# Attention and gated MLP on one core: from the eighth pair on, row maxima without a bias pass on TensorE; the attention run of a pair unbroken; setup off VectorE; maxima written in place

## The chip, the core and the metric

The kernel runs on one NeuronCore of a Trainium2 chip. Its five engines (TensorE, VectorE, ScalarE, GpSimd, and SyncE, which here issues all transfers) run their own instruction queues in order and wait for one another by semaphores. The metric is the device time of one launch in microseconds (us). In the profile TensorE is PE (its weight loads PEld), VectorE DVE, ScalarE ACT, GpSimd POOL, SyncE SP.

## The reference

Causal attention with a position bias over 8 batches x 8 heads, 576 positions, head size 64, and behind it a gated MLP with a depthwise convolution of width 3.

```python
scores = scale * np.matmul(q, k.transpose(0, 1, 3, 2))
cum = np.cumsum(np.maximum(s, 0.0), axis=-1)
bias = -(cum[:, :, :, None] - cum[:, :, None, :])
scores = np.where(causal, -1000000000.0, scores + np.minimum(bias, 0.0))
scores = scores - np.max(scores, axis=-1, keepdims=True)
attn = np.exp(scores)
attn = attn / (np.sum(attn, axis=-1, keepdims=True) + 1e-09)
x = attn @ v                                  # heads side by side: (8, 576, 512)
h = np.maximum(x @ w_in, 0.0)                 # w_in (512, 1024)
conv_out[:, t] = sum over k of conv_w[k] * h[:, t + k - 1]
out = (h * sigmoid(conv_out)) @ w_out         # w_out (1024, 512)
```

`cum` does not fall along a row, so under the causal mask the bias of a query is `cum[key] - cum[query]`.

## The kernel before

**Pairs.** Two heads make a pair; there are 32 pairs (p = 0 to 31), four to a batch. The two heads lie in partitions 0 to 63 and 64 to 127 and are worked on by matmuls with 64 rows each, two side by side. For each pair:

- `qk`, `hi`, `lo`: q and k are loaded and split into a leading and a rest part (`raw` to `s`); ACT or DVE makes the first, POOL the second.
- `sh0` to `sh3`: q k^T with queries in partitions, in four pieces of 288, 288, 448+64 and 320+192 columns, each for two heads in two of the six PSUM banks `ps0` to `ps5` (`sh_mm`). A first pass multiplies q and k, a second pass adds the keys' bias (tile `eb` times `ek`). `mx` (`sh_max`) takes the row maxima on DVE, in 12 operations per pair: a plain reduction, or a custom operation that adds a mask and takes the maximum, followed by a read of its accumulator. The custom operation writes its sum to a bf16 tile `junk` that nobody reads.
- `tn`, `rt`, `ds`: the maxima are transposed on PE, and go by DMA into a row of `eq`.
- `sc0` to `sc3`: k q^T with keys in partitions, three passes on the split parts and one of bias and maximum (`eq`, `ek`); `ex` is the exponential on ACT, `mk` the causal mask on POOL (from pair B0 = 9 on; before it, extra small matmuls on PE add the mask).
- `ad`, `sum`, `pv`: column sums and attn times v, on PE in column tiles of 32.
- `gd`, `inv`, `ri`, `rb`, `nm`: the sums (128 x 144) go through ACT, a reciprocal on DVE, a DMA to DRAM, a DMA that spreads them over the partitions, and a product on DVE. Then `xh`, `xl` split x.

**MLP.** For each batch and half, `h` (12 matmuls each, L1315) and after ReLU, convolution and gate `o` (6 matmuls each, L1442). At the start w_in and w_out arrive as words of 8 bytes and are rebuilt on DVE, ACT and POOL.

**Order.** A scheduler inside the kernel (`Sched.play`) plays all tasks through once, with a cost for each, a due time (its formula plus a table of shifts, `DUE`) and the free buffers, and writes each engine's instructions in the order that comes out. For pairs from B0 on the list `ORDER` says in which order the PE tasks of a pair follow; `sh` of the next pair runs with `sc` of this one. A "|" in it ends a burst, and only between bursts may `h`, `o` and `tn` come in. PE changes between three ways of tiling: 64 rows (`sh`, `sc`), 32 columns (`sum`, `pv`, `tn`) and the full array (`h`, `o`).

**The other way to maxima.** The code has a second way for pairs from `RB` on (`late` in `pair`): the row `cum` of both heads is loaded into all partitions (`rw`, 128 x 2 x 576, one tile), POOL cuts off keys behind the query in it (`cut_off`, five selects per pair, of which that for tau = 3, 2, 1 waits for the maxima of tau + 1, because they write over the columns that these read), and `sh_max` adds that row to q k^T. Its PE pass with `eb` and `ek` is left out. With RB = 32 no pair takes it.

Of the kernel before, what the change touches and what calls it, by code (L numbers as in the profile page):

```python
# [1556 lines left out]
```

## Time and profile before

| | |
|---|---|
| median of 3 runs | 785.36 us (784.96 to 786.0) |
| profiled execution | 785.74 us, of which the span in the trace is 783.9 us |
| PE busy | 746.5 us, 95% |
| DVE busy | 561.4 us, 72% |
| ACT busy | 446.7 us, 57% |
| POOL busy | 334.4 us, 43% |
| moved by DMA | 62.33 MB |

Busy is the time in which at least one instruction of the engine ran. Matmuls overlap, so what one costs is read from the distance of starts, not from its own duration. A row of the timeline has its start, its length, the engine, the line, the operation, output and inputs, and in brackets the idle time before it with what ended it.

### The profile page before, as it was taken

The page shows a single profiled execution, that of the slowest core. Times are in us where ns is not written, and L with a number is a line of the kernel's source. Part 1 is how long each engine was busy: PE and PEld are TensorE (multiplying, and loading weights), DVE is VectorE, ACT ScalarE, POOL GpSimd, SP SyncE. Part 2 cuts the span into 40 slices and gives each one's busy share as a digit, 9 for nine tenths or more (in the row PEclk, how much of TensorE's full clock was granted, in tenths as well). Part 3 has the DMA queues.
Part 4 walks back from the last instruction along what each step waited for, and adds up shares of the span by engine and source line. Part 5 has one row for each costly group of instructions (what it writes and reads, how often), then busy time and mean ns, then how long its engine had stood idle before and what let it go on. Part 6 is the DMA issues. An engine that isn't in the chain of part 4 may idle for free.

```text
span 783.9 us, 19117 instructions
## 1 busy us (share of the span) xinstructions
PE 746.5 (95%) x7528; PEld 616.8 (79%) x7528; DVE 561.4 (72%) x1355; ACT 446.7 (57%) x908; POOL 334.4 (43%) x456
## 2 busy tenths in 40 slices
PE   0898999999999999999999999999999999999998
PEld 0677788888888788787878788787887878888986
DVE  8986889753778685777776867777777768866532
ACT  4655565645656465665655566666655655644533
POOL 3343644412444455456254444545335354342311
PEclk9998999999999999999999999999999999999999
DMA  8364541211122312122222221222222121111001
GB/s 279 124 202 141 160 127 55 65 47 60 37 84 81 98 45 73 53 84 82 68 68 82 82 77 53 83 84 83 68 73 84 57 53 50 51 33 34 27 28 42
DMA packets 45466, 62.33 MB, mean 80 GB/s; under 512 B 5312, under 2 KB 30208, under 8 KB 45376
## 3 DMA queue, kind: packets, MB, share of 16 engines
q1 hardware_dynamic: 45376, 61.10, 25.3%
q8 instruction: 59, 0.97, 0.5%
q14 instruction: 31, 0.25, 0.1%
HBM read 48.83 MB, written 12.09 MB: 78 GB/s over the span
## 4 chain that ended last, share of the span: by engine, by line
PE 81%; DVE 7%; DMA 5%; issue 3%; ACT 2%; POOL 1%; SPq 1%; DVEq 0%; ACTq 0%; POOLq 0%
PE ps L1315 26%; PE ps L1442 25%; PE ps L1109 12%; PE pv L1163 9%; PE ps L991 6%; PE ps L1217 3%; DMA ri_d<-rs 2%; DMA rb<-ri_d 2%; DVE junk L1022 1%; DMA ht<-w_out 1%; ACT pt L1126 1%; DVE ad L1180 1%; DVE ct L1371 1%; DVE rs L1241 1%; DVE r L1013 1%
## 5 line engine op out<-in xcount | busy, mean ns | idle before, releaser
L1315 PE MATMUL ps<-x,wi 128*128 128x258 f32 (+1 forms) x1536 | 222.1, 300 | 0.9 <-ACT pt L1126 0.5
L1315 PEld LDWEIGHTS ps<-x,wi 128*128 128x128 f32 x1536 | 211.0, 189 | 8.1 <-issue 2.3
L1442 PE MATMUL ps<-wo,u 128*128 128x512 f32 x768 | 196.9, 402 | 0.5 <-ACT pt L1126 0.3
L1126 ACT ACTIVATE pt<-ps,less 128x288 f32<-128x288 f32 (+1 forms) x256 | 137.1, 591 | 78.7 <-PE ps L1109 76.1
L1385 POOL TENSOR_TENSOR u<-ct,u 128x512 fp32r<-128x512 f32 x64 | 84.5, 1321 | 219.8 <-ACT u L1380 167.2
L1352 DVE SCALAR_TENSOR_TENSOR ct<-ht,cw_sb,ct 128x320 f32<-128x320 f32 (+3 forms) x256 | 137.0, 542 | 50.2 <-ACT ct L1338 45.5
L1442 PEld LDWEIGHTS ps<-wo,u 128*128 128x128 f32 x768 | 138.6, 188 | 33.2 <-issue 3.0
L1109 PE MATMUL ps<-s 64*128 64x288 f32 (+4 forms) x1152 | 118.3, 309 | 2.0 <-ACT pt L1126 0.8
L1138 POOL TENSOR_SCALAR_AFFINE_SELECT pt<-pt 128x128 f32<-128x128 f32 x230 | 64.1, 302 | 116.0 <-ACT pt L1126 113.4
L1109 PEld LDWEIGHTS ps<-s 64*128 64x128 f32 (+1 forms) x1152 | 82.7, 177 | 25.1 <-issue 7.6
L1022 DVE CUSTOM_DVE_ANT_0 junk<-ps,mask 128x448 bf16<-128x448 f32 (+3 forms) x184 | 77.8, 423 | 29.4 <-PE ps L991 14.6
L1326 ACT ACTIVATE ht<-ps 128x257 f32<-128x257 f32 (+1 forms) x128 | 52.3, 410 | 78.5 <-PE ps L1315 75.1
L897 POOL TENSOR_TENSOR s<-raw,s 128x1152 fp32r<-128x1152 f32 x31 | 85.0, 2743 | 23.3 <-issue 13.2
L1163 PE MATMUL pv<-pt,v 128*32 128x448 f32 (+4 forms) x1536 | 94.0, 391 | 0.0
L1163 PEld LDWEIGHTS pv<-pt,v 128*32 128x32 f32 x1536 | 51.6, 111 | 40.0 <-issue 28.6
L991 PE MATMUL ps<-s 64*128 64x288 f32 (+4 forms) x384 | 65.5, 319 | 10.4 <-DVE s L891 3.9
L1180 DVE TENSOR_TENSOR ad<-ad,pt 128x192 f32<-128x192 f32 (+2 forms) x131 | 63.9, 541 | 8.0 <-POOL pt L1138 7.8
L1338 ACT ACTIVATE ct<-ht,cw_sb 128x320 f32<-128x320 f32 (+1 forms) x123 | 65.6, 535 | 5.6 <-ACT ht L1326 0.4
L991 PE MATMUL ps<-ek,eb 64*128 64x288 f32 (+4 forms) x384 | 59.7, 321 | 4.9 <-ACT ek L926 4.9
L1013 DVE TENSOR_REDUCE r<-ps 128x1 f32<-128x288 f32 (+4 forms) x136 | 51.0, 431 | 18.5 <-PE ps L991 18.3
L1371 DVE TENSOR_TENSOR ct<-ct,ht 128x640 f32<-128x640 f32 (+1 forms) x64 | 53.1, 830 | 11.8 <-ACT ct L1365 11.7
L1365 ACT ACTIVATE ct<-ct 128x640 f32<-128x640 f32 (+1 forms) x64 | 43.6, 681 | 24.1 <-DVE ct L1352 23.9
(94 smaller groups left out, 861.3 us busy)
## 6 DMA issues: line engine op xcount, KB each, us to landing
raw<-qk SPq DMA_DIRECT2D x32, 576.0 KB
v<-vp SPq DMA_DIRECT2D x32, 320.0 KB
rb<-ri_d SPq DMA_DIRECT2D x64, 144.0 KB
out<-ob SPq DMA_DIRECT2D x32, 256.0 KB
w<-w_in SPq DMA_DIRECT2D x8, 512.0 KB
ri_d<-rs SPq DMA_DIRECT2D x32, 72.0 KB
ht<-w_out SPq DMA_DIRECT2D x8, 256.0 KB
w<-w_out SPq DMA_DIRECT2D x4, 512.0 KB
```

Of the source, the lines that this page charges most:

```text
L897: tt_on(e)(st[:, i, :], R_t[raw.slot][:, i], st[:, j, :].bitcast(F32), op=ALU.subtract)
L991: nc.tensor.matmul(dst[j], l, m, start=(k == 0), stop=(k == 1 or late))
L1022: nc.vector.tensor_tensor_reduce(out=junk[:, 0 : c1 - c0], in0=bank(pb, o, o + c1 - c0), in1=add_, scale=1.0, scalar=acc if c0 else -3.0e3 ...
L1109: nc.tensor.matmul(d, l, m, start=(k < 2), stop=(k >= len(steps) - 2 or (t == L and k < 2)), skip_group_check=t == L,)
L1126: nc.scalar.activation(PT_t[pts[j].slot][:, o : o + w], bank(pb, 0, w), AF.Sigmoid, bias=less, scale=0.125,)
L1163: nc.tensor.matmul(pvt[gs, o0 : o0 + c1 - c0], vt[0:jt, t, gs], PT_t[pts[g // 2].slot][0:jt, O_T[t] + c0 : O_T[t] + c1], start=(t == 0), s ...
L1180: tt_on(e)(acc, pt[:, P:S] if t == 1 else acc, pt[:, O_T[t] : O_T[t] + W_T[t]], op=ALU.add,)
L1315: nc.tensor.matmul(bank(hb, 0, XW[hf]), l, r, start=(k == 0), stop=(k == len(seq) - 1))
L1338: nc.scalar.activation(o, src, AF.Copy, scale=w)
L1352: nc.vector.scalar_tensor_tensor(cc[:, lo:hi], h_[:, sh + lo : sh + hi], cw_sb[:, 3 * f + k : 3 * f + k + 1], cc[:, lo:hi], op0=ALU.mult, ...
L1385: tt_on(e)(uu[:, 1, i, :], C_t[ct.slot][:, i, k0:hw], uu[:, 0, i, :].bitcast(F32), op=ALU.subtract)
L1442: nc.tensor.matmul(bank(pb, 0, DM), l, r, start=(fp == 0 and k == 0), stop=(fp == NF // 2 - 1 and k == len(seq) - 1),)
```

## The change

Seven things change.

1. `RB` goes from 32 to 7: pairs 7 to 31 take their maxima the other way. PE loses for these 25 pairs the pass with `eb` and `ek` (300 of its matmuls), DVE works only with the custom operation, now with the float32 row `rw` as its second input, POOL gets five selects per pair and SP a load of 576 KB per pair, and `rt` adds an offset from a small table `off`.
2. `ORDER` loses its bars and puts `sh0`, `sh1` first: from pair 9 on the attention run of a pair is one burst, with no `h`, `o` or `tn` inside.
3. The custom operation writes its sum over the PSUM bank it reads; `junk` is gone.
4. The setup (constants, masks, pads of `ek`) moves from DVE to POOL and ACT.
5. The sums are folded by DMA from 128 x 144 (eight rows in use) to 128 x 9 before the reciprocal (`fo`, two DMAs per pair), and stored from there.
6. `ek` has two buffers (NE = 2) and one more for the early pairs; `ad` alternates the heads; the two taps of the convolution are tasks of their own.
7. The scheduler's costs and the whole table `DUE` are new, so the order of everything is.

```diff
-NE = 3
+NE = 2
...
-SWITCH = 0.105
+SWITCH = 0.2, 0.095
...
-RB = 32
-ORDER = ("sum", "pv", "sc0", "sh0", "|", "sc1", "sh1", "|", "sc2", "sh2", "|", "sc3", "sh3")
+RB = 7
+ORDER = ("sh0", "sh1", "sum", "pv", "sh2", "sc0", "sc1", "sh3", "sc2", "sc3")
...
     def c_clear(e):
-        nc.vector.memset(ones, 1.0)
-        nc.vector.memset(ncz, 0.0)
...
+        g = nc.gpsimd
+        g.memset(ones, 1.0)
+        g.memset(cols, 0.0)
...
     def c_pads(i):
         def run(e):
-            t = EK_t[i].bitcast(F32)
-            nc.vector.memset(t, 0.0)
-            for j in range(2):
-                nc.vector.memset(t[D * j : D * j + NB + 2, 0:S], -1.0)
-                nc.vector.memset(t[D * j : D * j + NB + 1, S:FW], NEG)
+            v = ident[:, 0:1]
+            for k, (c0, c1) in enumerate(((0, S), (S, FW))):
+                nc.scalar.activation(
+                    EK_t[i][:, c0:c1], bass.AP(v.tensor, v.offset, [v.ap[0], (0, c1 - c0)]),
+                    AF.Identity, bias=cols[:, k : k + 1], scale=0.0,
+                )
...
-                            out=junk[:, 0 : c1 - c0], in0=bank(pb, o, o + c1 - c0),
+                            out=bank(pb, o, o + c1 - c0), in0=bank(pb, o, o + c1 - c0),
...
+        def fold(e):
+            for j in range(2):
+                nc.sync.dma_start(
+                    rc_t[D * j : D * j + D], rs_t[j : j + 97 : 32].rearrange("g (k c) -> g k c", k=16)
+                )
+
+        t_fold = add(f"fo{p}", [("SP", 0.8)], [t_grd], tq, fold, uses=[ri], nbytes=30000)
+
         def inverse(e):
-            nc.vector.reciprocal(rs_t, rs_t)
+            nc.vector.reciprocal(rc_t, rc_t)
```

The order of instructions shows it at two places. First PE, in the middle of the program, before: the end of `sc0`, then `sh0` of the next pair with its second pass (`ek`, `eb`), 12 matmuls of `h`, and `sc1` (L1109 is `sc`, L991 `sh`, L1315 `h`; a row 128x288 stands for one head).

```order
L1109 MATMUL ps0_65<-eq0_87,ek1_85 128x288
L1109 MATMUL ps1_66<-eq0_87,ek1_85 128x288
L991 MATMUL ps2_67<-s0_82 128x288
L991 MATMUL ps4_69<-s0_82 128x288
L991 MATMUL ps2_67<-ek2_86,eb_113 128x288
L991 MATMUL ps4_69<-ek2_86,eb_113 128x288
L1315 MATMUL ps5_70<-x0_93,wi_78 128x322 x12
L1109 MATMUL ps0_65<-s1_83 128x288
L1109 MATMUL ps1_66<-s1_83 128x288
```

The same engine in the changed program, in the run of one pair: the end of `sc0`, `sc1` in two other banks, `sh3` of the next pair in a bank of `sc0`, and `sc2` (L1142 is `sc`, L1024 `sh`).

```order
L1142 MATMUL ps2_67<-eq0_85,ek1_84 128x288
L1142 MATMUL ps3_68<-eq0_85,ek1_84 128x288
L1142 MATMUL ps4_69<-s0_81 128x288
L1142 MATMUL ps5_70<-s0_81 128x288
...
L1142 MATMUL ps4_69<-eq0_85,ek1_84 128x288
L1142 MATMUL ps5_70<-eq0_85,ek1_84 128x288
L1024 MATMUL ps2_67<-s1_82 128x320
```

The second pass is gone, and so is the MLP work between the pieces; a bank is written again after one other piece. In the whole program the stretches with one way of tiling fall from 225 (96 of them with 64 rows) to 143 (66), when `tn` is counted with the full array.

Second POOL, before: masks of the probabilities (L1138), one sum (L1180), splits of x (L1281) and the split of the next q and k (L897).

```order
L1138 AFFINE_SELECT pt1_92<-pt1_92 64x64
L1180 TENSOR_TENSOR ad_96<-pt0_91 128x448
L1281 TENSOR_TENSOR x0_93<-rb_95,x0_93 128x322
L1281 TENSOR_TENSOR x1_94<-rb_95,x1_94 128x258
L1138 AFFINE_SELECT pt0_91<-pt0_91 128x128 x2
L1138 AFFINE_SELECT pt1_92<-pt1_92 128x128 x2
L1385 TENSOR_TENSOR u1_1860<-ct1_106,u1_1860 128x512
L897 TENSOR_TENSOR s0_82<-raw0_80,s0_82 128x1152
```

And in the changed program, around one pair: L982 is a select of the loaded row, L930 the split, L1434 a split of the MLP, L1173 a mask of the probabilities.

```order
L982 AFFINE_SELECT rw_87<-rw_87 128x2x128
L982 AFFINE_SELECT rw_87<-rw_87 128x2x64
L930 TENSOR_TENSOR s0_81<-raw0_79,s0_81 128x1152
L982 AFFINE_SELECT rw_87<-rw_87 128x2x128
L1434 TENSOR_TENSOR u0_1666<-ct2_108,u0_1666 128x512
L1173 AFFINE_SELECT pt0_91<-pt0_91 128x128
L982 AFFINE_SELECT rw_87<-rw_87 128x2x128
L1173 AFFINE_SELECT pt1_92<-pt1_92 128x128
L982 AFFINE_SELECT rw_87<-rw_87 128x2x128
```

The five selects stand spread over POOL's queue, among its long operations.

## Rows read from the trace of the kernel before

**Rows 1.** Windows: stretch, length, busy us (count) of PE, PEld, DVE, ACT, POOL; PEclk, DMA.

```profile
0.00:25.00 25.00, 4.96 (x44) 3.92 (x45) 22.13 (x56) 12.31 (x20) 10.07 (x17) 1.00 0.82 266
50.00:75.00 25.00, 23.34 (x368) 18.29 (x364) 19.85 (x51) 12.27 (x29) 9.97 (x9) 0.86 0.57 180
200.00:700.00 500.00, 494.59 (x4839) 402.97 (x4838) 368.89 (x928) 295.76 (x602) 239.41 (x371) 1.00 0.24 70
```

**Rows 2.** Timeline of the start: first bias row, on DVE, and PE's first second pass.

```profile
10.05 0.54 DVE L641 TENSOR_SCALAR pt<-pt 64x576 f32<-64x576 f32 x1
...
21.07 0.61 PE L991 MATMUL ps<-ek,eb 64*128 64x288 f32 x2 [4.89 <-ACT ek L926]
```

**Rows 3.** Timeline of PE in one pair's run, in the middle.

```profile
407.27 0.29 PE L991 MATMUL ps<-ek,eb 64*128 64x288 f32 x2
407.49 1.67 PE L1442 MATMUL ps<-wo,u 128*128 128x512 f32 x6
...
409.87 0.30 PE L991 MATMUL ps<-ek,eb 64*128 64x288 f32 x2
410.00 0.78 PE L1109 MATMUL ps<-s 64*128 64x448 f32 x6
...
411.31 0.36 PE L991 MATMUL ps<-ek,eb 64*128 64x448 f32 x2
411.51 0.19 PE L991 MATMUL ps<-s 64*128 64x64 f32 x2
411.54 0.27 PE L991 MATMUL ps<-ek,eb 64*128 64x64 f32 x2
411.65 0.68 PE L1109 MATMUL ps<-s 64*128 64x320 f32 x6
```

**Rows 4.** Chain that ended last, in order of time: start, length, what.

```profile
343.07 1.60 PE ps L1442 x6
...
346.40 1.65 PE ps L1315 x12
348.04 1.40 PE ps L1442 x6
...
349.56 1.45 PE ps L1315 x12
```

**Rows 5.** Groups by shape: count, busy us, mean ns, idle before and its releaser.

```profile
L897 POOL TENSOR_TENSOR s<-raw,s 128x1152 fp32r<-128x1152 f32 x31 | 85.0, 2743 | 23.3 <-issue 13.2 <-ACT s L891 8.0 <-DMA rb<-ri_d 1.1
L1126 ACT ACTIVATE pt<-ps,less 128x288 f32<-128x288 f32 x128 | 56.1, 497 | 50.5 <-PE ps L1109 50.1
L1138 POOL TENSOR_SCALAR_AFFINE_SELECT pt<-pt 128x128 f32<-128x128 f32 x184 | 55.4, 315 | 116.0 <-ACT pt L1126 113.4
L1241 DVE RECIPROCAL rs<-rs 128x144 f32<-128x144 f32 x32 | 33.6, 1050 | 23.7 <-ACT rs L1236 23.7
L1022 DVE CUSTOM_DVE_ANT_0 junk<-ps,mask,r 128x288 bf16<-128x288 f32 x64 | 33.0, 516 | 32.8 <-PE ps L991 27.5 <-DVE r L1022 0.7 <-ACT ek L926 0.2
L1022 DVE CUSTOM_DVE_ANT_0 junk<-ps,mask 128x448 bf16<-128x448 f32 x46 | 28.6, 622 | 12.2 <-PE ps L991 4.8 <-ACT pt L1126 4.2 <-DVE r L1022 0.9
L1180 DVE TENSOR_TENSOR ad<-pt 128x448 f32<-128x448 f32 x21 | 20.9, 1013 | 0.0
L1022 DVE DVE_READ_ACCUMULATOR2_ANT r<- 128x1 f32 x248 | 20.4, 82 | 0.0
L1013 DVE TENSOR_REDUCE r<-ps 128x1 f32<-128x448 f32 x18 | 10.3, 616 | 1.9 <-PE ps L991 1.9
```

**Rows 6.** Timeline of an early pair's four score pieces without MLP work between, PE.

```profile
56.53 0.79 PE L1109 MATMUL ps<-s 64*128 64x448 f32 x6
...
58.09 1.09 PE L1109 MATMUL ps<-s 64*128 64x320 f32 x6 [0.17 <-ACT pt L1126]
```

**Rows 7.** Timeline of SP: store of the reciprocals and the spread that waits for it.

```profile
405.40 0.35 SPq L1246 DMA_DIRECT2D ri_d<-rs  x1
...
407.09 1.29 SPq L1255 DMA_DIRECT2D rb<-ri_d  x2
```

More of the change, by code (lines that the diff above doesn't have):

```diff
@@ L46 @@
 LO1 = 4.0
-LAND = 0.65
+LAND = 0.85
+LEAD = {"PE": 0.0, "DVE": 0.08, "ACT": 0.1, "POOL": 0.04, "SP": 0.0}
+AFTER = {"PE": 0.2, "DVE": 0.12, "ACT": 0.14, "POOL": 0.1}
 ADD_ = 0.0
@@ L376, in play @@
                 else:
-                    post(now + dur + (0.2 if e == "PE" else 0.07), "done", t)
+                    post(now + dur + AFTER[e], "done", t)
             if not events:
@@ L466 @@
     cw_sb = const.tile([P, NF * 3], F32, name="cw_sb")
-    junk = const.tile([P, W_T[1]], BF16, name="junk")
     wi = const.tile([P, 2, NC, DF], F32R, name="wi")
@@ L572, in c_clear, with c_clear2 @@
     def c_clear(e):
-        nc.vector.memset(ones, 1.0)
-        nc.vector.memset(ncz, 0.0)
-        nc.vector.memset(tab[:, 0:1], 0.0)
-        nc.vector.memset(onehot, 0.0)
-        nc.vector.memset(onehot[:, 2:3], 1.0)
-        nc.vector.memset(less, -EK)
+        g = nc.gpsimd
+        g.memset(ones, 1.0)
+        g.memset(cols, 0.0)
+        for j in range(2):
+            g.memset(cols[D * j : D * j + NB + 2, 0:1], -1.0)
+            g.memset(cols[D * j : D * j + NB + 1, 1:2], NEG)
+        g.memset(ncz, 0.0)
+        g.memset(tab[:, 0:1], 0.0)
+    def c_clear2(e):
+        g = nc.gpsimd
+        g.memset(onehot, 0.0)
+        g.memset(onehot[:, 2:3], 1.0)
+        g.memset(less, -EK)
         for r8 in R8_t:
-            nc.vector.memset(r8, 0.0)
-        nc.vector.memset(mrow, 0.0)
-        nc.vector.memset(mask, 0.0)
+            g.memset(r8, 0.0)
+        g.memset(mrow, 0.0)
+        g.memset(mask, 0.0)
     def c_ident(e):
@@ L627 @@
     t_s = add("s", [("SP", 1.2)], [], -200, lambda e: nc.sync.dma_start(s_sb, s), nbytes=147456)
+    t_clear = add("clear", [("POOL", 1.3)], [], -191, c_clear)
     t_ident = add("ident", [("POOL", 1.0)], [], -190, c_ident)
-    t_clear = add("clear", [("DVE", 1.3)], [], -190, c_clear)
-    t_tab = add("tab", [("DVE", 0.3)], [t_ident, t_clear], -189.5, c_tab)
-    t_mrow = add("mrow", [("POOL", 4.0)], [t_clear, t_tab], -188.4, c_mrow)
-    t_tri = add("tri", [("POOL", 0.6)], [t_clear], -188.3, c_tri)
-    t_pads = [add(f"pads{i}", [("DVE", 1.4)], [], -189 + i, c_pads(i)) for i in range(NE)]
+    t_tab = add("tab", [("POOL", 0.3)], [t_ident, t_clear], -189.5, c_tab)
+    t_hot = add("hot", [("POOL", 1.3)], [], -189.4, c_clear2)
+    t_unit = add("unit", [("POOL", 0.35)], [t_ident], -189.3, c_unit)
+    t_mrow = add("mrow", [("POOL", 3.2)], [t_hot, t_unit], -188.4, c_mrow)
+    t_tri = add("tri", [("POOL", 0.3)], [t_hot], -188.3, c_tri)
+    t_pads = [
+        add(f"pads{i}", [("ACT", 1.0)], [t_clear, t_ident], -187 + i, c_pads(i)) for i in range(len(EK_t))
+    ]
     t_eb = add("eb", [("ACT", 0.72)], [t_tab], -188, c_ind(EB_t))
@@ L637 @@
     ]
-    t_hot = t_clear
     def cum_chain(e):
@@ L874, in pair @@
         late = p >= RB
-        raw, sb, vb, ek, eq = buf("raw"), buf("s"), buf("v"), buf("ek"), buf("eq")
+        extra = not late and RB < NP and p % 3 == 2
+        raw, sb, vb, ek, eq = buf("raw"), buf("s"), buf("v"), buf("eke" if extra else "ek"), buf("eq")
         lanes = [slice(D * j, D * j + D) for j in range(2)]
@@ L1173, in pair @@
         if ad:
-            for j in range(2):
-                t_ad = None
-                for t in range(1, NT):
+            t_ads = [None, None]
+            for t in range(1, NT):
+                for j in range(2):
+                    t_ad = t_ads[j]
                     def pre_add(e, j=j, t=t):
@@ L1190, in pair @@
                     )
-                added.append(t_ad)
+                    t_ads[j] = t_ad
+            added = t_ads
         def sums(e):
@@ L1257, in spread @@
                 )
-        t_rb = add(f"rb{p}", [("SP", 1.35)], [t_ri], tq, spread, alloc=[rb], uses=[ri],
+        t_rb = add(f"rb{p}", [("SP", 1.25)], [t_ri], tq, spread, alloc=[rb], uses=[ri],
                    nbytes=438000)
@@ L1343, in moe_h, with tap @@
                       [t_relu, t_cw], h_tag(b, hf, f) + 0.1, center, uses=[ht, ct])
-            def tap(e, i=i, f=f):
-                h_ = H_t[ht.slot][:, i, :]
-                cc = C_t[ct.slot][:, i, :]
-                for k in (0, 2):
+            t_tap = t_c
+            for k in (0, 2):
+                def tap(e, i=i, f=f, k=k):
+                    h_ = H_t[ht.slot][:, i, :]
+                    cc = C_t[ct.slot][:, i, :]
                     sh = hf + k - 1
@@ L1356, in tap @@
                     )
[L1358 to L1359 removed]
+                t_tap = add(f"t{'ab'[k // 2]}{b}.{hf}.{f}", [("DVE", 0.205 + hw / 0.96e3, True)], [t_tap],
+                            h_tag(b, hf, f) + 0.1, tap, uses=[ht, ct])
+            taps.append(t_tap)
         tg = h_tag(b, hf, 2 * fp + 1) + 0.2
```

60 lines of the change are left out of this document (32 added, 28 removed), and 153 rows, old and new, of the table DUE.

## The prediction, on record before the run

> **What bounds the kernel now.** I read the windows first, because a share of 95% over the whole span hides which stage is full. In the 500 us from 200 to 700 PE is busy for 494.6 us, DVE for 369, ACT for 296, POOL for 239 [rows 1]. So there a microsecond that PE no longer has to work is a microsecond of the kernel, unless PE then stands and waits, and the 5.4 us in which it is idle are all that it visibly waits today. The first 25 us are another stage: PE is busy for 4.96 us, DVE for 22.1. The timeline of the start says why. The chain that makes the bias rows starts on DVE at 10.05 us, and PE's first pass with `ek` comes at 21.07, after ACT has levelled a row that had to travel through DRAM [rows 2]. From 50 to 75 us PE is at 23.3 of 25, but its granted clock is 0.86 on average: part of that stretch ran at the lower of the two levels, 1.2 GHz, while DVE worked for 19.9 of the 25 us [rows 1]. In the middle, then, PE's own work bounds the kernel, and at the start DVE and what follows it.
>
> **The sum goes against the profiled execution**, 785.74 us, which is 0.4 above the median of 785.36. About 0.2% (1.6 us) is what a measurement of this kernel can tell from no change.
>
> **The second pass.** Two heads run side by side, so what a pass costs is the distance from its start to the next start. For 288 columns that is 410.00 - 409.87 = 0.13 us, for 448 it is 411.51 - 411.31 = 0.20, for 64 it is 411.65 - 411.54 = 0.11 [rows 3]. A pair has 288 twice, 448, 64, 320 and 192. For the last two, which lie between, I take 0.15 and 0.12. That makes 0.84 us per pair, and 25 pairs give 21 us; if the 64 columns cost only what the first pass of 64 does (411.54 - 411.51 = 0.03), it is 19. Pairs 7 and 8 also lose 28 small mask matmuls: at half of 0.11 us each some 1.5 us, at nothing 0; I take 1.
>
> **The switches of tiling.** Six matmuls of `o` take 1.40 us when PE stays with the full array and 1.60 when 64-row work follows; twelve of `h` take 1.45 and 1.65 [rows 4]. So a switch to 64 rows costs 0.20 us. The other way, the last pass before `o` takes 407.49 - 407.27 = 0.22 instead of 0.13: 0.09 us [rows 3]. The order has 96 stretches of 64 rows before and 66 after, 129 others before and 77 after: 30 x 0.20 + 52 x 0.09 = 10.7, say 11 us. For switches between columns and rows I have no row and use the same two prices; at nothing for them it would be 8 us.
>
> **What the unbroken run costs.** Before, each piece was followed by MLP work in most cases, and a bank had time to be emptied. Now the run goes `sh2`, `sc0`, `sc1`, `sh3`, `sc2`, `sc3` with six banks of which each piece takes two. I count from the start of `sc0`. Its four passes of 288 end at 0.5 us and those of `sc1` at 1.05. The last matmuls take 0.30 us themselves [rows 3], so ACT can start at about 0.8, and two exponentials of 0.50 us [rows 5] free the banks of `sc0` at 1.8. `sh3` wants them at 1.05: 0.75 us of waiting. The custom operations on `sh2` take 0.62 + 0.08 us for 448 columns [rows 5], perhaps 0.3 for 64, all of it twice: 2.0 us, so its banks are free at 2.3, and `sc2`, which would come at about 2.1, waits 0.15 more. That is 0.9 us per burst. An early pair has four score pieces in a row already, and there the fourth waits visibly for 0.17 us, and its first matmuls take 1.09 us, where the same six take 0.68 in the middle [rows 3, 6]: 0.6 us for one such reuse, so the size is right. In the order, 17 of the 23 bursts have six banks. In the other six a bank is still kept by `o`, so that `sc1` waits for `sc0` and `sc3` for `sc2` too; I put 1.9 us there. 17 x 0.9 + 6 x 1.9 = 27; the 5.4 us idle of today are mostly waits of this kind and go: +21 us net. From below it is about nothing (0.3 us per burst, as now), from above 2.0 us in every burst, +41. I take the middle, since the row of the early pair is the nearest.
>
> **Setup off DVE.** If POOL needs as long for its memsets as DVE did, nothing is gained; if the bias chain starts almost at once, 9 us. POOL is busy for only 10 of the first 25 us [rows 1] and the MLP's splits can wait, so I take 5. What covers it is that ACT, which now fills the pads, was busy for 12 of these 25 us.
>
> **The fold.** DVE loses 1.05 us per pair and gets back perhaps 0.2 [rows 5]: 27 us over 32 pairs, of which only those of the early pairs count, where DVE is what PE waits for: 7 x 0.85 = 6 us, at best 8 with the drop of the clock avoided, at least 0. I take 4. For it the chain from the sums to x gets one more DMA. Store to spread takes 407.09 - 405.40 = 1.69 us [rows 7], so the chain grows by 1.69 - 0.85 = 0.85 us. MLP work covers it in the middle; where x is late at the ends of the 8 batches it is 7 us at most.
>
> **What costs nothing.** Custom instead of plain reductions: 0.62 + 0.08 against 0.62 us for 448 columns [rows 5], for some 66 operations under 10 us, on a DVE with 131 of 500 us free. Writing over the bank instead of `junk`: no row shows it; if it cost nothing or as much again as a read of the accumulator, 0.08 us, that is 24 us on DVE at most, under the same cover. The selects: 125, each on twice the 128 columns that take 0.315 us [rows 5], so 40 to 79 us on a POOL with 261 of 500 us free. The loads: 25 x 576 KB = 14.7 MB, on DMA engines that are busy for a quarter [rows 1].
>
> One place shows that the engines are not as free as that. On 448 columns DVE takes 1.01 us with both inputs in SBUF and 0.62 with one in PSUM [rows 5]. The Trainium skill (GPSIMD Engine Reference, section 1, Specifications) says that GpSimd's interfaces to SBUF are shared with VectorE and that they get into each other's way when a DVE instruction has two SBUF inputs. The 0.4 us agree with it. By that rule POOL's added selects and memsets slow the rebuilding of the weights at the start, and the 4 us of the fold are lost: 768 instead of 764. By the rows alone the fold's relief stays. I stay with the rows, since most selects come after the weights are done.
>
> **The sum:** -21 - 1 - 11 + 21 - 5 - 4 = -21; 785.7 - 21 = 764.7, less the 0.4 to the median: 764 us.
>
> **Rivals.**
>
> *The waits stay hidden* (0.17). If ACT and DVE empty the banks as fast as PE comes back, the run costs 0.3 us per burst, about what is idle now: 785.4 - 42 + 2 = 745 us. For it speaks that ACT is busy for only 59% in the middle [rows 1]; against it, the early pair [rows 6].
>
> *POOL comes too late* (0.09), the case on the slower side. The select for tau = 3 waits for the four maxima of `sh0` and `sh1`, and the custom operations on `sh2` wait for it, on an engine that works in order. A split of 2.74 us [rows 5] ahead of that select holds up DVE, `sh2` keeps its banks, and `sc2` stands. From 0.9 us more in each of the 23 bursts on, the gain of 21 us is gone; half a split each time, 1.4 us, gives 785.4 - 21 + 32 = 796 us. POOL is free for half of the middle [rows 1] and the sums and `pv` give it 3 us, which speaks against it.
>
> *x comes late or the start does not move* (0.10). The longer chain at 8 batch ends adds 7 us, or the 9 us of start and fold fail: 771 to 773 us.
>
> *Given back in full* (0.04). The bursts cost 1.9 us everywhere: 23 x 1.9 - 5 = 39, and 785.4 - 42 + 39 = 782; with a little of the last rival within 0.2% of before.
>
> **How the numbers follow.** The forecast (0.60) has its own range of 752 to 776: the waits between 0.4 and 1.4 us per burst. With the hidden waits below and the rivals near it above, 745 to 780 holds 8 in 10. Faster: 0.60 + 0.17 + 0.10 = 0.87; no change 0.04; slower 0.09.
>
> **What would show it.** `ps<-ek,eb` has 84 matmuls, not 384, and PE's count falls by some 330. The first of them starts near 16 us. DVE's reciprocals shrink to about 0.2 us. PE shows idle time before `sh3` and `sc2`, released by the exponentials and by the custom operations, in all some 25 us in the middle; the groups of six `o` at 1.60 us become rare. I am wrong if that idle time is near nothing or over 40 us, if POOL's selects are named as what DVE waited for in most bursts, or if `h` waits for x at the ends of batches.

## The result, and the profile after

| | before | changed | ratio, 95% interval |
|---|---|---|---|
| first comparison, medians of 8 runs each | 785.68 us | 776.89 us | 0.9893 [0.9865, 0.9921] |
| the changed kernel again, later (6 runs) | 785.52 us | 777.98 us | 0.9892 [0.9862, 0.9923] |

The change gives 8 to 9 us, not 21. The profiled execution of the changed kernel took 780.09 us, 2 to 3 more than its median; below, differences between traces are taken from it, and times of experiments go against 777.5 us, between the two medians.

Busy times of the whole span, from the page of the changed kernel:

```profile
PE 726.9 (93%) x7200; PEld 603.6 (78%) x7200; DVE 550.1 (71%) x1475; ACT 443.8 (57%) x880; POOL 369.3 (47%) x557
```

The windows that answer to [rows 1]:

```profile
0.00:25.00 25.00, 4.54 (x38) 3.50 (x40) 17.45 (x34) 13.04 (x24) 15.79 (x35) 1.00 0.88 270
50.00:75.00 25.00, 22.24 (x392) 16.54 (x393) 21.20 (x57) 15.72 (x35) 12.11 (x9) 1.00 0.60 188
200.00:700.00 500.00, 480.96 (x4608) 396.13 (x4607) 371.74 (x1056) 291.58 (x573) 264.63 (x444) 0.99 0.30 93
```

In the middle PE is now idle for 19 us of 500 (before: 5.4), and in the first 25 us it does as little as before, although DVE has 4.7 us less to do. The timeline of the start, from DVE, SP, ACT and PE, says what took DVE's place (it answers to [rows 2]):

```profile
3.85 0.54 DVE L673 TENSOR_SCALAR pt<-pt 64x576 f32<-64x576 f32 x1 [3.85 <-DMA pt<-s]
...
6.17 0.57 DVE L680 TENSOR_SCALAR pt<-pt,v 64x576 f32<-64x576 f32 x1
...
5.76 3.97 SPq L759 DMA_DIRECT2D w<-w_in  x1
9.85 1.32 SPq L696 DMA_DIRECT2D grid_d<-pt  x1
11.27 0.54 SPq L698 DMA_DIRECT2D rest_d<-pt  x1
11.91 0.55 SPq L718 DMA_DIRECT2D ncr_d<-v  x1
12.50 1.01 SPq L719 DMA_DIRECT2D cum_d<-pt  x1
13.60 1.02 SPq L912 DMA_DIRECT2D raw<-qk  x2
15.20 0.66 SPq L945 DMA_DIRECT2D ek<-grid_d  x2
...
20.66 0.78 ACT L959 ACTIVATE ek<-ek,nbt 74x576 fp32r<-74x576 f32 x1 [1.72 <-DMA ek<-grid_d]
...
21.49 0.61 PE L1024 MATMUL ps<-ek,eb 64*128 64x288 f32 x2 [10.68 <-ACT ek L959]
```

The chain starts 6.2 us earlier and its row is ready at 6.74. But SP stands in the issue of a weight load until 9.73, stores the row at 9.85, then does two stores that the new way to maxima needs (`ncr_d`, `cum_d`) and two loads of q and k, and only then the load of `ek`. PE begins at 21.49; before it was 21.07. The same store, load and levelling (ACT) in the kernel before:

```profile
12.79 0.49 SPq L664 DMA_DIRECT2D grid_d<-pt  x1
...
16.23 0.67 SPq L912 DMA_DIRECT2D ek<-grid_d  x2
...
20.25 0.78 ACT L926 ACTIVATE ek<-ek,nbt 74x576 fp32r<-74x576 f32 x1 [4.39 <-DMA ek<-grid_d]
```

So of the 6.2 us the store keeps 2.9, the load 1.0, and the levelled row nothing: from store to load takes 5.35 us instead of 3.44, from load to levelling 5.46 instead of 4.02. The DMA engines are nearly full in this stretch in both traces: in the three windows of 5 us from 5 to 20 us the view gives them a busy share of 1.01, 1.02 and 0.86 before, and 1.00, 1.08 and 0.98 after.

Groups by shape, answering to [rows 5]:

```profile
L1055 DVE CUSTOM_DVE_ANT_0 ps<-ps,rw,r 128x288 f32<-128x288 f32 x50 | 24.2, 521 | 1.2 <-POOL rw L982 1.1
L1055 DVE CUSTOM_DVE_ANT_0 ps<-ps,rw 128x448 f32<-128x448 f32 x50 | 30.4, 647 | 2.4 <-PE ps L1024 0.7 <-POOL rw L982 0.7
L1055 DVE DVE_READ_ACCUMULATOR2_ANT r<- 128x1 f32 x314 | 44.3, 141 | 0.0
L1287 DVE RECIPROCAL rc<-rc 128x9 f32<-128x9 f32 x32 | 6.8, 212 | 17.3 <-DMA rc<-rs 17.1 <-issue 0.2
L982 POOL TENSOR_SCALAR_AFFINE_SELECT rw<-rw 128x256 f32<-128x256 f32 x100 | 52.5, 525 | 109.2 <-DVE r L1055 63.2 <-DMA rw<-cum_d 38.7 <-DVE rc L1287 7.1
L1217 DVE TENSOR_TENSOR ad<-pt 128x448 f32<-128x448 f32 x33 | 22.4, 684 | 3.1 <-POOL pt L1173 3.1
```

**Where the time went, by stretches.** Matmuls of a pair's `sum` mark the pairs. Distances in us from the traces:

| | to pair 0's sum | to pair 8's sum | to pair 31's sum | rest | span |
|---|---|---|---|---|---|
| before | 38.2 | 163.7 | 502.8 | 79.2 | 783.9 |
| changed | 38.5 | 166.0 | 496.4 | 77.4 | 778.4 |

The order has 12 matmuls of `o` more in the second stretch (2.5 us) and 12 of `h` fewer in the last (1.7 us). Like for like the head is where it was, and all of the gain lies between pair 8 and pair 31. That stretch, by kinds of work, each from the distances of starts (waits go to the kind that stood in front of them):

| pair 8's sum to pair 31's sum | before | changed |
|---|---|---|
| `sh` | 47.7 | 30.5 |
| `sc` | 84.1 | 102.5 |
| `sum`, `pv`, `tn` | 80.3 | 81.2 |
| `h` (1020, then 1032 matmuls) | 143.2 | 144.5 |
| `o` (588, then 576 matmuls) | 147.6 | 137.6 |

The pass gives 17.2 us in `sh` and the waits of the run take 18.4 in `sc`; what is left, 7 us in `o` and 0.4 in `h` with the counts evened out, I put down to the changes of tiling that went; no run tests these alone. One burst with six banks shows the waits (timeline, PE, ACT and DVE):

```profile
288.61 0.53 PE L1024 MATMUL ps<-s 64*128 64x288 f32 x4
...
292.45 0.50 PE L1024 MATMUL ps<-s 64*128 64x448 f32 x4
292.78 0.64 PE L1142 MATMUL ps<-s 64*128 64x288 f32 x6
293.09 0.63 DVE L1055 CUSTOM_DVE_ANT_0 ps<-ps,rw 128x448 f32<-128x448 f32 x1
...
293.64 1.68 ACT L1161 ACTIVATE pt<-ps,less 128x288 f32<-128x288 f32 x4 [0.36 <-PE ps L1142]
...
294.19 0.80 PE L1024 MATMUL ps<-s 64*128 64x320 f32 x3
...
294.58 0.14 DVE L1055 DVE_READ_ACCUMULATOR2_ANT r<- 128x1 f32 x1
...
294.78 0.39 PE L1142 MATMUL ps<-s 64*128 64x448 f32 x1
...
297.14 1.30 PE L1362 MATMUL ps<-x,wi 128*128 128x322 f32 x7
```

`sh3` (294.19) gets its banks as the exponentials on `sc0` end, and `sc2` (294.78) its own as the maxima of `sh2` end, at 294.58 + 0.14 = 294.72. The burst takes 297.14 - 288.61 = 8.53 us. The smallest that its pieces ever take, each taken from some burst, add up to about 7.75.

### The profile page after: what moved, and what is told of

Same layout as the page of the kernel before. It is cut to its first block, busy times and chain, and to the rows that moved or that the text cites. A ratio compares the mean times of both kernels' runs of the same rounds, so it can differ in the third digit from the quotient of the medians.

```text
span 778.4 us, 19056 instructions
## 1 busy us (share of the span) xinstructions
PE 726.9 (93%) x7200; PEld 603.6 (78%) x7200; DVE 550.1 (71%) x1475; ACT 443.8 (57%) x880; POOL 369.3 (47%) x557
## 3 DMA queue, kind: packets, MB, share of 16 engines
q1 hardware_dynamic: 50874, 73.94, 30.6%
## 4 chain that ended last, share of the span: by engine, by line
PE 65%; DVE 11%; DMA 9%; issue 3%; ACT 3%; SPq 2%; POOL 1%; DVEq 0%; POOLq 0%; ACTq 0%
PE ps L1491 22%; PE ps L1362 22%; PE ps L1142 9%; PE pv L1198 6%; DMA rb<-ri_d 3%; PE ps L1024 3%; PE ps L1255 3%; DMA ri_d<-rc 3%; DVE ct L1400 2%; DVE ad L1217 2%; DVE ps L1055 2%; DMA rc<-rs 1%; ACT pt L1161 1%; DVE ct L1420 1%; DMA ht<-w_out 1%
## 5 line engine op out<-in xcount | busy, mean ns | idle before, releaser
L1400 DVE SCALAR_TENSOR_TENSOR ct<-ht,cw_sb,ct 128x319 f32<-128x319 f32 (+3 forms) x256 | 144.7, 581 | 66.9 <-ACT ct L1385 64.4
L1491 PE MATMUL ps<-wo,u 128*128 128x512 f32 x768 | 187.6, 397 | 0.1
L1434 POOL TENSOR_TENSOR u<-ct,u 128x512 fp32r<-128x512 f32 x64 | 84.0, 1312 | 152.4 <-ACT u L1429 122.6
L1142 PE MATMUL ps<-s 64*128 64x288 f32 (+4 forms) x1152 | 119.5, 310 | 11.3 <-ACT pt L1161 5.5
L1055 DVE CUSTOM_DVE_ANT_0 ps<-ps,rw 128x64 f32<-128x64 f32 (+4 forms) x250 | 102.7, 455 | 38.0 <-POOL rw L982 18.1
L982 POOL TENSOR_SCALAR_AFFINE_SELECT rw<-rw 128x256 f32<-128x256 f32 (+1 forms) x125 | 62.8, 511 | 109.2 <-DVE r L1055 63.2
L930 POOL TENSOR_TENSOR s<-raw,s 128x1152 fp32r<-128x1152 f32 x31 | 84.9, 2739 | 44.6 <-DVE s L924 29.7
L1142 PEld LDWEIGHTS ps<-s 64*128 64x128 f32 (+1 forms) x1152 | 90.1, 181 | 20.3 <-ACT pt L1161 10.1
L1373 ACT ACTIVATE ht<-ps 128x321 f32<-128x321 f32 (+1 forms) x128 | 52.8, 413 | 73.3 <-PE ps L1362 73.0
L1173 POOL TENSOR_SCALAR_AFFINE_SELECT pt<-pt 128x128 f32<-128x128 f32 x230 | 69.6, 326 | 32.5 <-ACT pt L1161 30.8
L1198 PEld LDWEIGHTS pv<-pt,v 128*32 128x32 f32 x1536 | 50.0, 111 | 42.4 <-issue 30.6
L1024 PE MATMUL ps<-s 64*128 64x288 f32 (+4 forms) x384 | 59.2, 346 | 10.7 <-DVE s L924 4.1
L1385 ACT ACTIVATE ct<-ht,cw_sb 128x256 f32<-128x256 f32 (+1 forms) x121 | 64.5, 534 | 5.6
L1142 PE MATMUL ps<-eq,ek 64*128 64x288 f32 (+2 forms) x360 | 58.0, 303 | 0.0
L1024 PEld LDWEIGHTS ps<-s 64*128 64x128 f32 x384 | 35.8, 197 | 27.7 <-ACT pt L1161 8.6
```

The costliest lines, as they stand in the source:

```text
L930: tt_on(e)(st[:, i, :], R_t[raw.slot][:, i], st[:, j, :].bitcast(F32), op=ALU.subtract)
L1024: nc.tensor.matmul(dst[j], l, m, start=(k == 0), stop=(k == 1 or late))
L1055: nc.vector.tensor_tensor_reduce(out=bank(pb, o, o + c1 - c0), in0=bank(pb, o, o + c1 - c0), in1=add_, scale=1.0, scalar=acc if c0 else -3 ...
L1142: nc.tensor.matmul(d, l, m, start=(k < 2), stop=(k >= len(steps) - 2 or (t == L and k < 2)), skip_group_check=t == L,)
L1173: nc.gpsimd.affine_select(out=reg, in_=reg, pattern=[[1, dg]], compare_op=ALU.is_ge, fill=0.0, base=0, channel_multiplier=-1,)
L1198: nc.tensor.matmul(pvt[gs, o0 : o0 + c1 - c0], vt[0:jt, t, gs], PT_t[pts[g // 2].slot][0:jt, O_T[t] + c0 : O_T[t] + c1], start=(t == 0), s ...
```

## Experiments

Kernels with "before" in their names are the kernel before with an edit; all others are the changed kernel with one. Where the order of tasks is edited, all other instructions stay in the order that the scheduler gave.

### The start: after_again, sp_rows_first, setup_dve, rows_before_qk

> The changed kernel once more, unaltered, beside the three runs below. Expected 777 us, between 773 and 781, the spread seen so far. It is what the other three are compared with.

It took 777.98 us and is the second line of the first table.

```diff
 # sp_rows_first
+    move(["grid", "rst", "dr0", "cw", "wi4", "save"], "qk2")   # places these ahead of task qk2
 # rows_before_qk
+    move(["grid", "rst", "dr0"], "save")
+    move(["eq0"], "wi1h")
 # setup_dve: memsets, tab, unit on nc.vector, pads of ek as before, ahead of the chain
-        g = nc.gpsimd
+        g = nc.vector
```

> The changed kernel; in SP's queue the stores of the bias rows and the first pair's load of them stand ahead of two loads of weights and two of q and k. Theory (the 5 us of the setup were lost in SP's queue and behind the weights on the DMA engines): the first store starts near 6.8 us instead of 9.85, the first pass with ek near 16 instead of 21.5, and the kernel is 4 to 5 us faster than the changed one. Rival (the start is not on the path, since pairs 1 to 6 wait for DVE and for weights): the first pass comes as early, but the time moves by less than 1.5 us.

> The changed kernel with the memsets and the pads of ek back on DVE, in the same order. The forecast's term: 5 us slower than the changed kernel. Theory of the queue: the chain on DVE starts some 5 us later, but 3 us of that were waited for in SP's queue anyway, so the first pass with ek comes 2 to 3 us later and the time grows by no more than that. If the start is not on the path: 0.

> The changed kernel; in SP's queue the first load of the bias rows stands ahead of the stores of cum and of two loads of q and k, and on ACT its levelling ahead of a conversion of weights. Nothing is delayed by more than 2 us. Theory (the start is on the path and is held by SP's order): the first pass with ek starts near 19 us instead of 21.5 to 21.9 and the kernel is 2 to 3 us faster, 775. Rival (the start is not on the path): within 1 us of 777.5.

sp_rows_first took 782.08 us, 4 slower than after_again beside it. The store did start at 6.76, but the load waited for it until 12.57, on ACT the levelling of the row stood behind conversions of weights that now came later, and the first pass began at 22.09. setup_dve took 780.51, 2.5 slower; its first pass came at 24.61 instead of 21.9, and pair 0's sum moved from 38.1 to 41.6 us. That place alone says little: in pass_back and short_select, whose start is unaltered, it is 40.8 and 40.2. rows_before_qk took 778.87, no different within the scatter (the 14 executions of the changed kernel took 770.8 to 781.3 us). Its PE timeline:

```profile
18.35 0.61 PE L1024 MATMUL ps<-ek,eb 64*128 64x288 f32 x2 [7.70 <-ACT ek L959]
...
27.27 0.61 PE L1024 MATMUL ps<-ek,eb 64*128 64x288 f32 x2 [3.28 <-ACT ek L959]
```

The first pass starts 3.1 us earlier, and PE then waits 3.28 us for the row of the second pair. That row's load goes out when it did (20.27 us; 20.25 in the changed kernel), but on ACT its levelling moves from 23.31 to 26.44, behind a conversion of w_out whose words were now ordered 1.4 us later:

```profile
25.95 0.43 ACT L772 ACTIVATE ct<-ht 128x256 f32<-128x256 f32 x1 [6.48 <-DMA ht<-w_out]
26.44 0.77 ACT L959 ACTIVATE ek<-ek,nbt 74x576 fp32r<-74x576 f32 x1
```

Pair 0's sum comes at 41.7 us. The load of the first row went out at 14.75, only 0.45 us sooner, because SP waited 3.1 us for the store to land; the rest was gained between load and levelling (2.8 us instead of 5.5), now that the loads of q and k stood behind it. So a single row of the start is not the limit: each row has to pass SP, the DMA queues and ACT, and what was saved on the first was lost at the second. Whether the busy DMA engines set the pace of the whole start is a rival that no run tests. Taking DVE's memsets back costs 2 to 3 us, not 5; the granted clock of these runs is 0.990 on average and 0.995 in after_again, so part of that can be the clock.

### DVE's relief: no_fold, junk_back, before_dve

```diff
 # no_fold
-            nc.vector.reciprocal(rc_t, rc_t)
+            nc.vector.reciprocal(rs_t, rs_t)   # stored from rs_t, no folding DMAs
 # junk_back
-                            out=bank(pb, o, o + c1 - c0), in0=bank(pb, o, o + c1 - c0),
+                            out=junk[:, 0 : c1 - c0], in0=bank(pb, o, o + c1 - c0),
 # before_dve: both the other way round, in the kernel before
```

> The changed kernel without the fold: the reciprocal takes 128x144 again, and is stored from there. The forecast's term: 4 us slower than the changed kernel, up to 6, since DVE has some 27 us more work. Rival (the fold gains nothing, since the chain from the sums to x got a DMA longer, and early PE does not wait for DVE's total work): within 1.5 us, or up to 3 us faster.

> The changed kernel with the custom operation writing to the bf16 tile junk again. In place a read of the accumulator takes 141 ns, before 82. If that 0.06 us is due to the write in place: 15 us less on DVE, about half of it in the bursts, but covered there by the wait for ACT: 0 to 3 us faster. If the place of the write does nothing: within 1 us.

> The kernel before, in its own order, with the write in place and the fold. Nothing is left out. If what the two were worth in the changed kernel (10 and 8 us) holds here too: 18 us faster than before, 768. Theory (DVE's pace counts only where the maxima empty the banks in an unbroken run): 0 to 4 us faster, 781 to 785.

no_fold took 786.09 us (ratio to before 1.0017 [0.9997, 1.0036]): 8 us slower than after_again. It is not the head: from pair 0's sum to pair 8's it takes 163.8 us, no more than the changed kernel. The middle takes 499.4 instead of 496.4 (497.4 in after_again). The rest of the 8 us is not in its profiled execution, which was the fastest of its 12; the granted clock of its runs is 0.991 on average, and 0.995 in after_again, which by itself would be about 3 us.

junk_back took 787.45 us (1.0029 [1.0000, 1.0058]): 10 us slower, and neither theory had that. In its trace the stretch from pair 8's sum to pair 31's takes 507.4 instead of 496.4 us. The maxima of `sh0` and `sh1` of the same burst, on DVE, first in junk_back, then in the changed kernel:

```profile
289.62 0.45 DVE L1056 CUSTOM_DVE_ANT_0 junk<-ps,rw 128x288 bf16<-128x288 f32 x1
290.00 0.09 DVE L1056 DVE_READ_ACCUMULATOR2_ANT r<- 128x1 f32 x1
290.23 0.46 DVE L1056 CUSTOM_DVE_ANT_0 junk<-ps,rw 128x288 bf16<-128x288 f32 x1
...
290.87 0.52 DVE L1056 CUSTOM_DVE_ANT_0 junk<-ps,rw,r 128x288 bf16<-128x288 f32 x1 [0.17 <-DVE r L1056]
```

```profile
289.50 0.46 DVE L1055 CUSTOM_DVE_ANT_0 ps<-ps,rw 128x288 f32<-128x288 f32 x1
289.87 0.14 DVE L1055 DVE_READ_ACCUMULATOR2_ANT r<- 128x1 f32 x1
289.87 0.50 DVE L1055 CUSTOM_DVE_ANT_0 ps<-ps,rw 128x288 f32<-128x288 f32 x1
...
290.29 0.52 DVE L1055 CUSTOM_DVE_ANT_0 ps<-ps,rw,r 128x288 f32<-128x288 f32 x1
```

With one `junk` for all, each operation waits until the one before it has written: 0.61 and 0.64 us from start to start. The wait is one that the program makes: in the packed trace of junk_back 233 of the 314 operations stand behind a wait for a semaphore that DVE's own operations raise, and the last row of junk_back above shows the idle time that it leaves; in the changed kernel it is 72. In place, two neighbours write different banks, and the distance is 0.37 and 0.42. (`junk` also lies in SBUF and not in PSUM. No run separates the two; the semaphore waits are what the trace shows.) The durations (516 and 521 ns for 288 columns, [rows 5] and above) show nothing of it. So the write in place makes these steps of DVE's chain of maxima a third shorter, although the read of the accumulator becomes longer (141 instead of 82 ns).

before_dve took 803.59 us, 18 slower than before, for a reason that the expectation had overlooked. Among DVE's waits in it is

```profile
DVE rc L1245 <- DMA rc<-rs: 99.0, 30, 5.0
```

In the order of before the reciprocal stands right behind the sums, and now it waits there for the folding DMA, 3.3 us each time, with all of DVE's work queued behind it. In the changed order it stands later and waits 17.1 us in all. Of the 18 us, 12 come between pair 0's sum and pair 8's (175.9 instead of 163.7), and 6 up to pair 31's. So this run does not tell what the relief is worth in the old order; that is open.

### The pass: pass_back, before_no_pass, before_no_pass_dve

```diff
 # pass_back (operands of the first pass, over its result)
-                    for k in range(1 if late else 2):
+                    for k in range(2):
-                            nc.tensor.matmul(dst[j], l, m, start=(k == 0), stop=(k == 1 or late))
+                            nc.tensor.matmul(dst[j], l, m, start=(k == 0 or late), stop=(k == 1 or late))
 # before_no_pass
-                    for k in range(1 if late else 2):
+                    for k in range(1 if p >= 7 else 2):
```

> The changed kernel; each late piece of sh is multiplied twice, the second time over the first, so PE has the 300 matmuls of the removed pass again, at the same places. The forecast's term, if a pass costs its full distance of starts: 25 x 0.84 = 21 us slower than the changed kernel. Theory (in the unbroken run DVE and ACT empty the banks at their own rate, so PE's work there fills waits): 6 to 12 us slower. If the pass was wholly hidden: 0 to 3.

> The kernel before, in its own order, without the pass with eb and ek from pair 7 on: the bias is left out of the maxima, everything else is done. PE has the same 300 matmuls and 28 small ones less as the changed kernel. The forecast's first term: 25 x 0.84 = 21 us and 1 for the masks, 763 to 765. Rival (also in this order part of the pass fills a wait, as in the unbroken run, where it was worth 14): 12 to 16 us faster than before, 770 to 773.

> The kernel before, in its own order, without the pass from pair 7 on (the bias is left out of these maxima), with the write in place and the fold. What remains of the change is the unbroken run with its new order, the loaded row with POOL's selects, and the setup; so the changed kernel's 777.5 less this time is what these cost. By the forecast's terms (21 for the waits less 11 for the switches less 5 for the setup): this kernel at 772. Theory (the run costs more than that, 15 us or more): 757 to 763.

pass_back took 791.12 us, 14 more than the changed kernel, between the forecast's 21 and the theory's 6 to 12. The burst shown above takes 9.38 us in it: 0.84 more, exactly the forecast's price. So it is in seven of the sixteen bursts with six banks; the others change by -0.6 to +1.1 us (150.0 us together, 141.5 and 142.5 in the two traces of the changed kernel); the six with five banks take 68.0 us instead of 65.8 and 67.1, so there the pass fills waits.

before_no_pass took 770.16 us (0.9810 [0.9777, 0.9842]), 15 less than before. In its trace `sh` between pair 8's and pair 31's sums takes 30.6 us instead of 47.7, and all other kinds stay within 1 us: 17.1 us for 22 pairs, 0.78 each. The stretch before it is 3.1 us shorter, and the start came 2.6 later in that execution. PE stays full in the middle:

```profile
200.00:700.00 500.00, 494.45 (x4730) 397.35 (x4730) 381.37 (x948) 302.71 (x620) 244.46 (x374) 1.00 0.23 71
```

So the price of the pass was nearly right, 0.78 for 0.84. This run is also 7 us faster than the changed kernel, with the same matmuls: what else the change brings (the unbroken run, the loaded row with its selects, the setup, the fold, the write in place) costs some 7 us on balance. With its other edits this kernel shares the delay of before_dve and took 792.54 us, 11 less than before_dve: neither is fit for the sum that it was meant for.

### The waits: short_max, short_exp, short_both, short_select, short_taps

```diff
 # short_max, from pair 10 on
+                            add_ = add_[:, 0:16]                 # and as many columns of the bank
 # short_exp, from pair 10 on
-                        PT_t[pts[j].slot][:, o : o + w], bank(pb, 0, w), AF.Sigmoid,
+                        PT_t[pts[j].slot][:, o : o + D], bank(pb, 0, D), AF.Sigmoid,
 # short_select, from pair 10 on
+                        k = 4
 # short_taps, from the third batch on
+                        hi = lo + D
```

> The changed kernel; from pair 10 on each custom operation of the maxima works on 16 columns instead of 64 to 448, so the maxima are not those of the row. DVE loses about 75 us of work. Theory (DVE's emptying of the banks is half of the waits in the run): 8 to 15 us faster than the changed kernel. Rival (ACT's exponentials or POOL's selects hold the banks): 0 to 4 us faster.

> The changed kernel; from pair 10 on each exponential works on 64 columns instead of 288 to 512, so most of the probabilities are left out. ACT loses about 50 us of work. Theory (ACT's emptying of the banks of sc0 and sc1 is the other half of the waits): 6 to 12 us faster than the changed kernel. Rival (DVE alone holds the banks): 0 to 3 us faster.

> The changed kernel with the maxima on 16 columns and the exponentials on 64 columns at once, from pair 10 on; most of the work on rows and probabilities is left out. Theory (in a burst with six banks the wait for ACT before sh3 and the wait for DVE before sc2 cover one another, so that either alone gains little): a burst falls from 8.5 to 7.7 us, the kernel is 18 to 24 us faster than the changed one, 754 to 760. Rival (the two add up): 6.7 + 1.6 = 8 us, 769.

> The changed kernel; from pair 10 on each of POOL's selects in the loaded row works on 4 columns per head instead of 128, so keys behind the query are not cut off. POOL loses about 40 us of work. Theory (POOL is not what the banks wait for): 0 to 3 us faster than the changed kernel. Rival (DVE's maxima wait for the selects, 17 us in 27 waits in the trace, and PE for them): 8 us faster or more.

> The changed kernel; from the third batch on each of the two taps of the convolution works on 64 columns instead of 255 to 320, so the convolution is left out in most columns. DVE loses some 60 us of work, none of it on banks that the run waits for. Theory (PE waits for the maxima alone): the taps only stand ahead of the maxima at times, 1 to 3 us faster than the changed kernel. Rival (DVE's whole load, worked off in order, sets the pace): as much per microsecond of DVE as the short maxima, 5 to 8 us faster.

| | median, us | against 777.5 | the burst shown above | `sc`, pair 8's to 31's sum |
|---|---|---|---|---|
| short_max | 770.85 | -6.6 | 8.54 | |
| short_exp | 775.86 | -1.6 | 8.47 | |
| short_both | 770.09 | -7.4 | 8.16 | 90.6 |
| short_select | 773.82 | -3.7 | 8.54 | |
| short_taps | 775.71 | -1.8 | 8.54 | |

With four executions each, short_exp, short_select and short_taps can't be told from no change. short_max or short_exp alone leaves the burst at 8.5 us, both together bring it down to 8.16: in it the waits for ACT and DVE do cover one another. `sc` falls by 12 us to 90.6, so these two engines hold the banks. But the time falls by 7, not by 18 to 24. In its trace `sc` and `sh` lose 15 us in the middle, of which 6 come back in `sum`, `pv` and `tn` (87.2 us instead of 81.2). TensorE's clock may be another part: the four runs were granted 0.984, 0.991, 0.986 and 0.991, on average 0.7% less than in after_again, which by itself would be some 5 us, an estimate. The selects are named in 27 waits of DVE in the middle, 17.2 us, yet cost 4 us or less. The short taps take 42 us off DVE's busy time (550.1 to 507.9) and gain 2 us; the short maxima take off 59 (to 490.9) and gain 7.

### Six banks and a filler: six_banks, pv_split, pv_split_six

In the order six bursts have only five banks, because a sum of `o`, half of it done before the burst, keeps one.

```diff
 # six_banks: o's matmuls ahead of the burst move behind it (False), or the others ahead of it (True);
 # sc1 and sc3 get the freed bank, sh3 the banks of sc0, sc2 those of sh2, as in the other bursts
+    six(12, "o1.1.0", False)
+    six(15, "o2.0.0", False)
+    six(16, "o2.0.1", True)
+    six(26, "o4.1.1", True)
 # pv_split: pv's matmuls on the last three tiles of keys stand ahead of sh3
-                   pv_mm(range(NT)), alloc=[pv]
+                   pv_mm(range(2 if B0 - 1 <= p < NP - 2 else NT)), alloc=[pv]
```

> The changed kernel; in four of the six bursts that have only five banks, because a half-done sum of o keeps one, that sum is finished before the burst or begun after it, and the burst gets the sixth bank in the pattern of the other bursts. Nothing is left out. The four took 9.9, 10.9 to 12.5, 11.6 to 14.6 and 10.4 us in the profiles so far, 44 to 46 us together, and a burst with six banks takes 8.5. Theory (the kept bank is what makes them long): 8.5 each, so 10 us less, of which some is lost where PE has less to do before a burst: 7 to 10 us faster than the changed kernel, 768 to 771. Rival (they are long because DVE and ACT are late there with the work of the MLP): 0 to 3 us.

> The changed kernel; of the 48 matmuls of pv, those on the last three tiles of keys (some 1.1 us) stand behind sc1 and ahead of sh3, where PE waits for ACT and DVE, in 22 bursts. Nothing is left out. Theory (the waits in the burst are on the path): PE's own work fills the 0.85 us of a burst with six banks, less some 0.3 us for two more switches of tiling; 8 to 14 us faster than the changed kernel, 764 to 770. Rival (DVE and ACT set the pace over the whole period of a pair, so that a shorter burst is given back as a wait of h or o): 0 to 3 us, 775 to 778.

> The changed kernel with the split of pv and with the sixth bank in the four bursts of six_banks. Theory of the waits on the path: the bursts with five banks fall too, 10 to 18 us faster than the changed kernel, 760 to 768. Rival (pace of DVE and ACT): no faster than the split of pv alone, since the four shorter bursts gave nothing before.

The four bursts went from 9.90, 12.51, 11.62 and 10.36 us to 8.51, 10.39, 9.76 and 9.66, 6 us less, and `sc` from 102.5 to 93.4. That bears out the Trainium skill (Perfetto Trace Analysis, section Optimizing Tensor Performance, Matmuls), by which independent groups should go round through the banks so that ACT and DVE empty one while the next is filled: one bank fewer costs 0.7 to 2.1 us per burst here. But the kernel took 780.35 us, and the stretch from pair 8's sum to pair 31's is as long as before the edit (496.6 us). The time comes back one step later, as waits of `h` for ACT's ReLU (waits of PE, 200 to 710 us; first six_banks, then the changed kernel):

```profile
PE ps L1362 <- ACT ht L1373: 6.5, 3, 2.9
```

```profile
PE ps L1362 <- ACT ht L1373: 2.4, 2, 2.1
```

`h` takes 150.4 us instead of 144.5 and `sh` 32.7 instead of 30.5. pv_split took 779.61 us: the burst above takes 8.33 us in it, but `sum`, `pv` and `tn` take 86.5 us instead of 81.2, which fits its two more changes of tiling per burst. pv_split_six took 782.39. None of the runs that do all the work is faster than the changed kernel.

## Why the prediction was wrong

**Right:** the mechanism in the middle, and its sum nearly. The forecast had -18.5 (22 pairs x 0.84) - 11 + 21 = -8.5 us there; the trace has -17.2 for the pass, -7.4 for the tiling and +18.4 in `sc` and 0.9 in `sum`, `pv` and `tn`: -5.3. Where PE would wait, and for whom, came as predicted in the burst shown; 84 matmuls with `eb` are left, and the reciprocals take 0.21 us.

**The step that failed: the setup and the fold.** "I take 5" for the setup and "I take 4" for the fold, with some 3.5 for the pass and masks of pairs 7 to 9, were to come in the first 200 us; that stretch is 12 us short of them. For the setup the prediction looked at DVE's queue and not at what follows it: SP takes the row 3.1 us late, its store and its load take 3.4 us longer than before, and ACT has levelled it no sooner (20.66 us, before 20.25). rows_before_qk shows that freeing the first row moves the wait to the second. For the fold, "DVE is what PE waits for" in the early pairs was read from [rows 1], where DVE is busy for 20 of 25 us. But without the fold (no_fold) these pairs take no longer: 163.8 us from pair 0's sum to pair 8's, against 166.0 with it. PE's idle time between the first pass with `ek` and pair 8's sum is 8.6 us; it was 8.4 before. This is the rival "the start does not move" (771 to 773 us), held at 0.10; the time came out beyond it because the middle gave 5 us and not 8.5. The visible idle time of the middle, 19 us, and its places would have fitted the forecast.

**Mis-sized:** the switches, 7.4 us instead of 11. The waits were right by two errors that cancel. Against 7.75 us, the sixteen bursts with six banks wait 0.8 us in the median and 1.1 on average, where 0.9 was said; the six with five banks took 65.8 us, 3.0 each above that (one has a `sum` that is 1 us longer), where 1.9 was said. That makes 36 us instead of 27. But the trace gives 19 net, so the order of before had waited some 17 us too, most of it hidden behind matmuls that overlap, and not the 5.4 of visible idle time that were taken off.

**"What costs nothing" was wrong for the write in place:** not the 0.08 us per operation of the bounds, and no cover, but 0.2 us off each step in the chain of maxima. The unbroken run no longer hides that chain in full: some 60 us more on DVE (an estimate, 314 operations at 0.2) cost 10 us when the write is undone. Undoing the fold costs 8, of which its trace shows 3, in the middle. The two did not bring 18 us against before; they keep the new kernel from being that much slower.

**The Trainium skill on the shared port** (GPSIMD Engine Reference, section 1, Specifications) was set aside in the forecast. The mean of 1.01 us in [rows 5] hides two sizes. In the trace before, one addition of 448 columns on DVE, and the split on POOL beside it:

```profile
279.96 3.10 DVE L1180 TENSOR_TENSOR ad<-pt 128x448 f32<-128x448 f32 x1
```

```profile
279.63 2.95 POOL L897 TENSOR_TENSOR s<-raw,s 128x1152 fp32r<-128x1152 f32 x1 [0.52 <-ACT s L891]
```

Ten of the 21 such additions took 0.61 to 0.62 us, three 1.8 to 3.8. That agrees with the rule for POOL's operations with two inputs, and not for its selects: in the changed kernel, with 125 selects more, the mean fell to 0.68, and the additions that overlap with selects alone took 0.60 to 0.73 us. The 768 us that the rule was given for the start were nearer to the time, but not for that reason. It works in the middle instead, ahead of one of the worst bursts (11.62 us) of the changed kernel:

```profile
328.56 3.33 DVE L1400 SCALAR_TENSOR_TENSOR ct<-ht,cw_sb,ct 128x256 f32<-128x256 f32 x2
```

```profile
328.78 2.83 POOL L930 TENSOR_TENSOR s<-raw,s 128x1152 fp32r<-128x1152 f32 x1
```

Two taps that need 0.55 us each take 3.33 because POOL splits the next q and k at that moment, and the maxima of the burst at 330.1 stand behind them.

**Still open:** why the time falls by less than the bursts do (six_banks, short_both). The waits of `h`, `sum` and `pv` and the clock may each account for a part; their shares were not separated. Open too is what the DMA engines, nearly full from 5 to 20 us, leave to be gained at the start.

## What to carry to other kernels

Follow a row to its user through every queue that it passes, the transfers' queue first: an engine that is relieved 6 us earlier gains nothing when the row is then held up in the issue of another transfer, on busy DMA engines and behind other work on ACT. When buffers are refilled without other work between, the chain that empties them comes onto the path, and small things in it (the tile that an unread result goes to, an operation ahead of it that waits for a DMA) can be worth 10 to 18 us, as much as a pass on the busiest engine (14 to 15). What an undo costs in the new kernel is not what the part brought against the old one.
